# A new hand-out of queues, PSUM banks and alternate engines in a two-layer attention and MLP kernel

## The chip, the cores and the metric

The kernel runs on one core of a Trainium2 chip. A core has a matrix engine (TensorE, PE in the profile; its weight loads are listed apart as PEld), a vector engine (VectorE, DVE), a scalar engine (ScalarE, ACT), GpSimd (POOL) and SyncE (SP), which here only starts transfers. Each engine works through its own queue in the order in which the program filled it; between engines there are only semaphores. Matmul results land in PSUM, which the kernel uses as eight banks of 128 x 512 float32; everything else sits in SBUF.

The metric is the time of one execution on the chip, in microseconds (us).

## The reference

The input is x, 2048 rows of 512 numbers. Two layers follow each other, with the same weights in both, and each layer is

```python
x = x + attention(layernorm(x), wqkv, wo)   # 32 heads of 16, causal, a row sees itself and the 255 rows before it
x = x + gelu(layernorm(x) @ w1 + b1) @ w2 + b2   # 512 -> 1792 -> 512
```

All inputs and the output are bfloat16.

## The kernel before

**Tiling.** Rows are taken in tiles of 128 (tau = 0..31 over both layers) and in blocks of two tiles (b = 0..15; blocks 0 to 7 are the first layer, 8 to 15 the second). A block of the second layer can start as soon as the rows it needs have left the first, so the two layers overlap. The MLP works in ten jobs J of two or four tiles (`JOBS`, line 456): J0 and J1 have two tiles, J2 to J7 four, J8 and J9 two.

**One block of attention.** `lnq` and `kv` (lines 647 and 666) normalize two tiles, transpose them through a DMA, and project them: nodes named `q`, `k`, `v`, whose results leave PSUM through `qe`, `ke`, `ve`. The scores of a block come in ten visits (five in blocks 0 and 8), 150 in all: `sc` (line 740) fills four banks, two `ex` on ACT (line 747) take the exponential of two banks each and write 128 x 1024 into E, and `mk` (line 768) multiplies the edges of the window by a 0/1 mask. After half of the visits, `pv` (line 792) multiplies E by V, with the row sums as a 17th column. Its two banks are transposed to SBUF (`od`, line 801), the sums inverted (`rc`, 805), the rows divided by them (`nm`, 809), transposed again (`ot`, 815), and `op` (the output projection, through line 639) uses the result; `rs` (841) adds it to x. The second half of the visits feeds a second `pv`.

**One MLP job.** `m` nodes multiply by w1. For six of the fourteen columns of tiles the bias is added on DVE (`gb`, line 864) and ACT takes the gelu of two at once (`ga`, 867); for the other eight ACT adds the bias and takes the gelu straight from PSUM (`ge`, 872). `y` nodes multiply by w2; `xb` (880, POOL) and `ya` (884, DVE) add the bias and x.

**Names.** `pv3_1` is the second half of block 3, `sc4_2` is visit 2 of block 4, `y5` the second matmul of the MLP for tile 5. All matmuls against full 128-row weights are recorded under line 639.

**What sets the order.** The program first makes a list of 3080 nodes, in the order in which the lines stand. Three lists written out by hand then decide everything: `_ORDER` is the order in which nodes are put into their engines' queues (SP's DMAs among them), `_ALT` names the nodes that go to their second engine (DVE to POOL for `mk` and `nm`, DVE to ACT for `qe`, `ve`, `te`, POOL to DVE for `vp`), and `_BANKS` gives the PSUM bank of each allocation in turn:

```python
for i in _ALT:
    nodes[i]["eng"], nodes[i]["fn"] = nodes[i]["alts"][1]
for i in _ORDER:
    for g, k in nodes[i]["alloc"]:
        b = next(banks)
        gmap[g] = tuple(range(b, b + k))
```

`_Sched.op` adds the semaphore waits from the reads and writes of each node, bank by bank, so any order that respects them computes the same. Eighteen matmuls on zeros (`warm`, line 532) stand ahead of the first real work.

## Time and profile before

| | us |
|---|---|
| median of 3 runs | 454.1 (453.41 to 454.37) |
| the profiled execution | 453.76 |
| its span, first to last instruction | 451.9 |
| PE busy | 428.1 (95%) |
| ACT busy | 386.4 (85%) |
| DVE busy | 352.2 (78%) |
| POOL busy | 192.2 (43%) |
| PE busy in four stretches: 0 to 100, 100 to 136, 136 to 205, 205 to 452 | 94.85, 25.64, 64.49, 243.16 |

The profiled execution is 0.34 us under the median of the runs shown, and 1.86 us of it lie outside the span. Busy time of PE is counted from the start of a matmul to its modelled end; matmuls overlap, so a PE that is always busy is not yet one that could do no more. Times inside the kernel are counted from the start of the span.

### The profile page before, as it was taken

To read this page: it belongs to the slowest core of one execution; us is meant where nothing else is said; L and a number is where in the kernel's file an instruction comes from. 1 tells how busy PE (TensorE), PEld (TensorE's weight loads), DVE (VectorE), ACT (ScalarE), POOL (GpSimd) and SP (SyncE) were. 2 spreads that over 40 slices of the span, in tenths; PEclk is the share of its full clock that TensorE was granted. 3 is DMA by queue.
4 is the path that set the end of the run, shared out by engine and by line. 5 is a ranking of instruction groups with operands and counts; after the bars stand their busy time and mean duration, and the time that the engine had idled before them with its cause. 6 is when DMAs were issued, how large, how long until landed. Compare 5 with 4: busy or idle time off the path is not lost.

```text
span 451.9 us, 16895 instructions
## 1 busy us (share of the span) xinstructions
PE 428.1 (95%) x7579; PEld 229.2 (51%) x7579; DVE 352.2 (78%) x654; ACT 386.4 (85%) x458; POOL 192.2 (43%) x216
## 2 busy tenths in 40 slices
PE   8998999985879998899999999999999999999997
PEld 4555747543434553445455455455654464444673
DVE  6998699887775778984899877887887598756862
ACT  2998978987799999789998999999878989899633
POOL 4264635236432347632482744364243443526130
PEclk9999999999899999999999999999999999999999
DMA  8684611202300211310022031010232003002110
GB/s 243 190 176 122 166 33 26 43 10 25 82 14 1 24 26 41 73 28 0 15 43 51 0 63 32 10 42 3 64 51 60 1 4 83 10 1 69 60 46 25
DMA packets 47972, 23.25 MB, mean 51 GB/s; under 512 B 33180, under 2 KB 47900, under 8 KB 47900
## 3 DMA queue, kind: packets, MB, share of 16 engines
q1 hardware_dynamic: 47900, 22.17, 21.6%
q8 instruction: 60, 0.98, 1.0%
q14 instruction: 12, 0.10, 0.1%
HBM read 8.00 MB, written 2.10 MB: 22 GB/s over the span
## 4 chain that ended last, share of the span: by engine, by line
PE 73%; ACT 15%; DVE 6%; DMA 3%; issue 1%; SPq 1%; POOL 0%
PE ps L639 57%; ACT E L747 12%; PE ps L740 8%; PE ps L792 7%; DVE E L768 2%; DVE OD L801 1%; DMA Wqkv_sb<-in_A_wqkv_dram 1%; ACT gT L872 1%; DMA xnTA<-xn 1%; DMA xnTB<-xn 1%; ACT gT L867 1%; DVE xn L613 1%; DVE KT L673 0%; DVE stat L591 0%; ACT QT L582 0%
## 5 line engine op out<-in xcount | busy, mean ns | idle before, releaser
L747 ACT ACTIVATE E<-ps 128x1024 bf16<-128x1024 f32 x300 | 283.3, 1040 | 37.6 <-PE ps L740 37.2
L768 POOL TENSOR_TENSOR E<-E,mask 128x512 bf16<-128x512 bf16 (+2 forms) x96 | 103.1, 1088 | 92.4 <-ACT E L747 92.2
L639 PE MATMUL ps<-W_sb,gT 128*128 128x512 bf16 x448 | 118.1, 381 | 0.0
L639 PE MATMUL ps<-xnTB,W_sb 128*128 128x512 bf16 (+1 forms) x560 | 114.6, 337 | 2.4 <-ACT E L747 1.9
L768 DVE TENSOR_TENSOR E<-E,mask 128x512 bf16<-128x512 bf16 (+2 forms) x140 | 70.3, 527 | 10.0 <-ACT E L747 9.8
L639 PE MATMUL ps<-xnTA,Wqkv_sb 128*128 128x256 bf16 x512 | 74.7, 273 | 1.6 <-ACT E L747 0.5
L639 PEld LDWEIGHTS ps<-xnTB,W_sb 128*128 128x128 bf16 x560 | 50.8, 97 | 44.9 <-issue 4.7
L740 PE MATMUL ps<-QT,KT 32*128 32x128 bf16 (+3 forms) x1920 | 60.7, 232 | 8.5 <-DVE OD L801 2.8
L639 PEld LDWEIGHTS ps<-W_sb,gT 128*128 128x128 bf16 x448 | 39.3, 97 | 43.3 <-issue 3.6
L639 PEld LDWEIGHTS ps<-xnTA,Wqkv_sb 128*128 128x128 bf16 x512 | 46.6, 98 | 26.0 <-issue 5.6
L740 PEld LDWEIGHTS ps<-QT,KT 32*128 32x128 bf16 x1920 | 28.9, 93 | 59.5 <-ACT E L747 37.8
L801 DVE STREAM_TRANSPOSE OD<-ps 128x1024 f32<-128x1024 f32 x32 | 39.8, 1245 | 19.6 <-PE ps L792 19.2
L872 ACT ACTIVATE gT<-ps,b1T 128x512 bf16<-128x512 f32 (+1 forms) x80 | 43.5, 609 | 10.2 <-PE ps L639 9.9
L880 POOL TENSOR_TENSOR Xb<-X,b2all 128x512 f32<-128x512 bf16 x32 | 38.5, 1208 | 25.0 <-DVE X L884 25.0
L673 DVE TENSOR_TENSOR KT<-ps,parmask 128x1024 bf16<-128x1024 f32 x32 | 38.8, 1213 | 11.1 <-PE ps L639 10.7
L792 PE MATMUL ps<-E,Va 64*17 64x64 bf16 (+3 forms) x1920 | 41.2, 230 | 4.0 <-ACT E L747 1.7
L591 DVE BATCH_NORM_STATS2 stat<-X 128x6 f32<-128x512 bf16 x64 | 42.7, 677 | 1.9 <-DMA X<-in_A_x_dram 1.8
L864 DVE TENSOR_SCALAR gT<-ps,b1T 128x512 bf16<-128x512 f32 (+1 forms) x60 | 36.6, 630 | 7.6 <-PE ps L639 7.0
L792 PE MATMUL ps<-E,Vs 64*17 64x192 bf16 (+3 forms) x1920 | 42.0, 230 | 0.0
L639 PE MATMUL ps<-Wo_sb,OT 128*128 128x512 bf16 x128 | 39.6, 388 | 1.7 <-DVE OT L815 1.6
L809 POOL TENSOR_TENSOR Nb<-OD,Rc 128x512 bf16<-128x512 f32 x19 | 20.1, 1058 | 48.8 <-DVE Rc L805 40.6
L639 PE MATMUL ps<-Wqkv_sb,xnTA 128*128 128x512 bf16 x128 | 38.6, 385 | 1.3 <-ACT E L747 1.0
(50 smaller groups left out, 354.4 us busy)
## 6 DMA issues: line engine op xcount, KB each, us to landing
Vs<-Va SPq DMA_DIRECT2D x64, 68.0 KB, 2.1
W_sb<-in_B_w_dram SPq DMA_DIRECT2D x4, 512.0 KB, 6.4
out_dram<-X SPq DMA_DIRECT2D x16, 128.0 KB, 1.9
X<-in_A_x_dram SPq DMA_DIRECT2D x3, 512.0 KB, 7.2
Wqkv_sb<-in_A_wqkv_dram SPq DMA_DIRECT2D x4, 256.0 KB, 5.6
W_sb<-in_B_w_dram SPq DMA_DIRECT2D x1, 768.0 KB, 5.5
W_sb<-in_B_w_dram SPq DMA_DIRECT2D x2, 384.0 KB, 3.9
Wqkv_sb<-in_A_wqkv_dram SPq DMA_DIRECT2D x1, 512.0 KB, 7.3
```

Of the source, the lines that this page charges most:

```text
L591: add("dve", lambda e, B, t=t, k6=k6: e.bn_stats(stat6[:, k6, :], X[:, t, :]), reads=["X%d" % t], writes=["st%d" % k6], key="bs%d" % (k + j))
L639: r = e.matmul(ps[:, B[g][0], cols], lhsT, rhs, start=st, stop=sp)
L673: add("dve", lambda e, B, g=g, i=i: e.tensor_tensor(out=KT[:, kb, 2 * i : 2 * i + 2].rearrange("p c m a q -> p a (c m) q"), in0=ps[:, B[g] ...
L740: x = e.matmul(ps[:, bk[r], o : o + n], KT[rows, kb, c, m].rearrange("p a q -> p (a q)"), QT[rows, c, q : q + n], start=True, stop=True)
L747: add("act", lambda e, B, g_=g_, gi=gi: e.activation(E[:, 2 * gi : 2 * gi + 2, e0 : e0 + 512], ps[:, B[g_][0] : B[g_][0] + 2, :], AF.Exp, ...
L768: fn = lambda e, B: e.tensor_tensor(out=Ew, in0=Ew, in1=Mw, op=ALU.mult)
L792: x = e.matmul(ps[32 * r : 32 * r + VW, B[g][par], c % 2 * 2 * P + lo : c % 2 * 2 * P + hi], V[rows, (2 * b + m // 2) % VR, c * HC + 2 * r ...
L801: add("dve", lambda e, B: e.transpose(OD[:, s].rearrange("p a c q -> p (a c q)"), ps[:, B[g][0] : B[g][0] + 2, :]), reads=["ps:" + g], wri ...
L809: return e.tensor_tensor(out=Nb[:, s, :].rearrange("p (k a d) -> p a k d", a=2, d=Dh), in0=sums[:, :, :, 0:Dh], in1=rc[:, :, :, None].to_b ...
L864: add("dve", lambda e, B, g=g, fc=fc: e.tensor_scalar(out=gT[:, fc, c0 : c0 + M], in0=ps[:, B[g][0], 0:M], scalar1=b1T[:, fc : fc + 1], sc ...
L872: add("act", lambda e, B, g=g, fc=fc: e.activation(gT[:, fc, c0 : c0 + M], ps[:, B[g][0], 0:M], AF.Gelu_apprx_tanh, bias=b1T[:, fc : fc + ...
L880: add("pool", lambda e, B, t=t, xs=xs: e.tensor_tensor(out=Xb[:, xs, :], in0=X[:, t, :], in1=b2all[:], op=ALU.add), reads=["X%d" % t, "b2a ...
```

## The change

Only the three lists change; the nodes, their instructions and their shapes are the same. The change is described as giving all queues, banks and alternate engines in a new order, with the ports that VectorE and GpSimd share going to whoever is there first, and the warm-up matmuls keeping to free banks. The diff replaces all of `_ORDER` and `_BANKS` and most of `_ALT`; its first lines:

```diff
 _ORDER = [
-    14, 17, 0, 22, 33, 4, 7, 34, 18, 37, 1, 19, 13, 36, 26, 3, 46, 15, 8, 27, 9, 56, 35, 16, 41, 57, 20, 60, 39, 58,
...
+    14, 17, 22, 0, 4, 33, 34, 37, 18, 19, 26, 36, 46, 35, 7, 41, 1, 15, 13, 3, 8, 9, 27, 56, 57, 60, 58, 59, 61, 2,
...
 _ALT = [
-    60, 66, 74, 79, 108, 112, 120, 125, 164, 169, 184, 191, 210, 219, 336, 341, 369, 373, 377, 378, 383, 392, 397,
...
+    60, 62, 66, 69, 74, 79, 112, 120, 140, 169, 184, 197, 201, 206, 210, 215, 219, 239, 326, 336, 341, 377, 378, 383,
...
 _BANKS = [
-    0, 2, 3, 6, 4, 1, 7, 1, 3, 4, 6, 0, 1, 2, 6, 4, 5, 6, 2, 1, 0, 4, 6, 1, 2, 4, 0, 6, 2, 4, 1, 6, 2, 4, 5, 6, 0, 2,
...
+    0, 7, 2, 0, 4, 6, 1, 6, 7, 0, 2, 5, 4, 6, 0, 5, 0, 6, 2, 4, 5, 2, 0, 7, 4, 2, 0, 6, 2, 4, 0, 6, 2, 5, 4, 6, 0, 2,
...
```

Read as names, and counted by engine:

- PE's queue has the same 1615 nodes, 1501 of them in another place (mean distance 9 places); SP's the same 159, 118 of them in another place. The eighteen warm-up matmuls and the transposes between them stand as before.
- 150 nodes change engine. `mk`: 48 from DVE to POOL, 39 from POOL to DVE. `nm`: 16 from POOL to DVE, 3 back. `vp` (a 128 x 2 addition in the layernorm): 11 from POOL to DVE, 7 back. Evictions of `q`, `v` and `te` from PSUM: 14 from ACT to DVE, 12 from DVE to ACT. DVE then has 664 nodes for 654, POOL 204 for 212, ACT 438 for 440.

As a sample, PE's queue from the first visit of block 3 to the second `pv` of block 4, before (x4 stands for four nodes of one group in a row):

```
sc3_0 y2x7 op5x2 sc3_1 op4x2 y2x3 y3 sc3_2 y3x5 k6_0 sc3_3 y3 k6_0 y3 k6_0 y3 k6_0 sc3_4 y3x2 v11 y3 v10 y3
v10x2 y3 q6_0 sc3_5 v11 v10 v11x2 q6_0 pv3_0 sc3_6 q6_0x2 sc3_7 sc3_8 op6x2 op7x2 sc3_9 q6_1x2 k6_1x3 sc4_0 q6_1
k6_1 q6_1 pv3_1 sc4_1 sc4_2 v12 op7 op6x2 sc4_3 op7 v12x2 sc4_4 v12 v13x2 k7_0 v13 q7_0 v13 k7_0 q7_0 sc4_5
k7_0x2 q7_0x2 pv4_0 sc4_6 m2_3x4 m2_4x2 sc4_7 m2_4 m2_1 m2_4 sc4_8 m2_1x2 m2_5x3 m2_1 m2_5 sc4_9 m2_2x4 sc5_0
sc5_1 pv4_1
```

and after:

```
sc3_0 k5_1x4 y2x3 pv2_1 y2x6 sc3_1 y2x5 sc3_2 op4x4 v10x3 sc3_3 v10 op5x4 sc3_4 q6_0x4 k6_0 sc3_5 k6_0 y3x3
k6_0x2 sc3_6 y3x7 sc3_7 v11x4 pv3_0 sc3_8 q6_1 sc3_9 y3 q6_1 y3x3 q6_1x2 sc4_0 k6_1x4 sc4_1 pv3_1 sc4_2 sc4_3
v12x3 op6 v12 op6x3 sc4_4 op7x4 v13 sc4_5 v13x3 q7_0x4 sc4_6 k7_0x3 sc4_7 k7_0 pv4_0 sc4_8 sc4_9 m2_2x4 m2_5x4
m2_4x2 sc5_0 m2_4x2 m2_3x3 m2_1x4 sc5_1 m2_3 pv4_1
```

## The prediction

> **What bounds the kernel now.** I read the busy times first. PE is busy for 95% of the span and ACT for 85%, so both are candidates and an average can't choose between them.

> ```profile
> PE 428.1 (95%) x7579; PEld 229.2 (51%) x7579; DVE 352.2 (78%) x654; ACT 386.4 (85%) x458; POOL 192.2 (43%) x216
> ```

> Then I read the busy time by windows (length, then PE, PEld, DVE, ACT, POOL busy, granted clock, DMA share, GB/s). They show where PE is not busy.

> ```profile
> 11.30:22.60 11.30, 11.12 (x190) 6.36 (x190) 11.28 (x23) 10.65 (x13) 2.33 (x6) 1.00 0.68 190
> 101.70:113.00 11.30, 6.13 (x200) 3.82 (x200) 8.05 (x14) 8.46 (x10) 7.34 (x8) 1.00 0.21 25
> 113.00:124.30 11.30, 9.28 (x208) 4.90 (x208) 8.59 (x19) 8.54 (x10) 4.74 (x5) 0.85 0.39 83
> 316.40:327.70 11.30, 11.30 (x352) 6.83 (x351) 9.87 (x18) 10.10 (x11) 2.52 (x4) 1.00 0.27 64
> ```

> From 205 us on PE is busy 243.16 of 247 us: there the kernel is at PE's speed. Between about 98 and 135 us, in blocks 3 and 4, no engine is full, and right after it the clock's mean is 0.85. This is a pocket of waits. The chain of waits names them:

> ```profile
> 98.84 7.45 ACT E L747 x8
> 106.31 2.19 DVE E L768 x3
> 111.20 1.17 DVE OD L801
> 114.28 1.33 PE ps L639 x3
> 252.09 9.64 PE ps L639 x44
> ```

> The chain leaves PE, runs through exponentials, masks, the transpose of `pv3_1`, and comes back to PE in `op`. The last line is the other regime: 44 full matmuls in 9.64 us, 0.22 each. The timeline shows the pocket from inside:

> ```profile
> 105.29 2.59 POOL L768 TENSOR_TENSOR E<-E,mask 128x512 bf16<-128x512 bf16 x2
> 106.31 2.19 DVE L768 TENSOR_TENSOR E<-E,mask 128x768 bf16<-128x768 bf16 x3 [2.19 <-ACT E L747]
> 108.60 0.23 PE L792 MATMUL ps<-E,Va 64*17 64x128 bf16 x4 [1.11 <-DVE E L768]
> 112.50 0.40 PE L740 MATMUL ps<-QT,KT 32*128 32x192 bf16 x12 [1.50 <-DVE OD L801]
> 114.28 1.33 PE L639 MATMUL ps<-Wo_sb,OT 128*128 128x512 bf16 x3 [0.83 <-DVE OT L815]
> ```

> One of the three DVE masks ran 1.51 us instead of the usual 0.55: it began under a POOL mask and ended about 0.4 us after it. `pv3_1` waited 1.11 us for it, the next score visit 1.50 for the transpose of `pv3_1`, and `op` 0.83.

> **The change, part by part.**

> *Sums of work.* Prices come from the groups by shape. The net moves are 9 masks from DVE (0.39 to 0.62 us) to POOL (0.70 to 1.66), 13 `nm` from POOL (1.058) to DVE (0.691), 4 `vp` to DVE (0.16) and 2 evictions from ACT (0.61) to DVE (0.68). With the masks' shapes that adds 3.9 us to DVE, 1.7 to POOL and takes 1.2 from ACT. DVE's 3.9 lie beside PE, which is longer everywhere after 205 us; uncovered they would cost 3.9. DVE is full only early (11.28 of 11.3 us above), and up to `od1_0` its queue now holds 30.5 us by these prices against 32.5. I take nothing (0 to 3.9).

> *Entries into tiled matmuls.* When PE goes from a full matmul to `sc` or `pv`, it loses 0.095 us (0.311 between starts for 0.216). The new order has 147 such entries for 154: 0.7 us less. It is counted in the next sum.

> *Score visits.* PE and ACT hand over at 150 visits, and PSUM's eight banks hold two visits at most. So I cut PE's queue at each visit and compare PE's work up to the next (0.216 a full matmul, 0.33 a visit, 1.3 a `pv`, 0.095 an entry) with ACT's work between their exponentials (0.90 each, 0.57 a gelu from PSUM, 0.95 a merged one, 1.28 a table load). The larger counts. Example: between `sc4_1` and `sc4_2` PE has 0.33, ACT two exponentials: 1.8. Before, these sum to 435.7 us; with the first visit at 12.1 that is 447.8, and PE's last matmul really begins at 448.5. The method closes to 1 us. After, the sum is 435.3: a gain of 0.4 (a gain of 3.2 if neighbours are taken in pairs, a loss of 0.5 in threes).

> *The start.* Ahead of the first visit stand 7.7 us of PE work for 8.4, and a statistics instruction (0.68) moves behind the `ke` that the visit needs. Against it, `te1` goes to ACT (0.60 for 0.42). I take a gain of 0.5 (0 to 0.9). The warm-ups keep their places; a wait of theirs would be seen as a gap between them, and there is none: nothing.

> *The pocket.* By the visits, blocks 3 and 4 should take 21.2 + 21.5; they took 21.4 + 25.2. Thus 3.7 us are hand-overs that had too little work behind them. I measured that cover: PE work from the last score of a half to its `pv`, and from `pv` to the first `op` that needs it. Before, in us: `pv3_0` 3.8, `pv3_1` 2.3, `pv4_0` 3.3, `pv4_1` 1.6; `pv3_1` to `op` 0.9. After: 6.1, 3.2, 4.8, 5.3 and 2.0. The first needs two exponentials and a mask, 2.4 us, and more if ACT is behind; `pv3_1` with 2.3 waited 1.1, so it needed about 3.4. The second needs 1.25 + 0.35 + 0.69 + 0.70, so 3.0. What stays short is 0.2 and 1.0: 1.2 of the 3.7. Gain 2.5 (0 to 3.7). The transposes for J2 that SP starts behind `op7` need some 6 us (116.7 to 122.9 before) and get five visits, 9 us.

> *What gets tighter.* `pv7_0` has 2.5 us of cover for 3.4, `pv2_0` 3.5 for 4.9. If 3.4 is needed, 0.9 is lost at `pv7_0`. Four masks that `pv0_1` and `pv1_0` wait for go to POOL, each 0.4 to 1.1 us longer; the cover is 3.6 and 5.9, so I take 0.3 (0 to 6.6, below). 118 moved transfers have the same sizes; SP waits mostly for `xn`, which its order follows. A transfer that comes late shows as a transpose wait on PE, of which the old queue had 0.3 at a time; I take nothing (0 to 2).

> *The ports.* 29 DVE instructions before were stretched, by 17.3 us in all; 23 masks that began under a running POOL instruction ended as it did, plus their own time. [...] By the rows alone, POOL has 105 masks for 96, so at the same rate 17.3 becomes 18.9, off the path but for full stretches. I take nothing (a gain of 1.0, the stretch in the pocket, to a loss of 1.6).

> *Sum.* 453.76 - 0.4 - 0.5 - 2.5 + 0.9 + 0.3 = 451.6 for an execution like the profiled one, which lies 0.34 under the median; on the median 451.9.

> **The rivals.**

> *The pocket stays.* ACT or DVE, not the cover, sets the pocket, and the waits only change places. For it: ACT's busy 7.45 us in a row on the chain. Against it: ACT itself idles 2.8 of 11.3 us there. Then 2.5 are not won: 454.4, no change.

> *Masks on POOL end halves late (slower).* With ACT one visit behind, a half whose last masks are on POOL needs 1.8 + 1.8 + 1.9 = 5.5 us; two behind, 7.3. Of the halves that changed, `pv0_1` has 3.6, `pv1_0` 5.9, `pv5_1` 5.7 with one small mask, `pv15_1` 4.4. Two behind, they lack 3.7, 1.4, 0.4 and, as no visit stands behind `pv15_1`, 1.1 by its gelus: 6.6 us, 458.5. It decides once ACT is more than one visit behind when the last score is issued. For it: ACT is full at 12 to 34 us (10.65 of 11.3). Against it: two visits need all eight banks, which rarely leaves ACT two behind.

> *The pocket closes wholly.* No cover short anywhere, and `pv5_0`, `pv6_0` (8.5 and 7.4 us for 3.8 and 3.9) win some of the 4.5 us that PE idles between 136 and 205: 451.9 - 1.2 - 1.2 = 449.5, less up to 2.

> That the ports collide as often as before, against the change's description, is the loss of 1.6 above; it stays inside the first rival's reach and gets no time of its own.

> **How the numbers follow.** Forecast 0.43, pocket stays 0.17, masks late 0.24, closes wholly 0.16. About 0.2%, 0.9 us, is what a measurement of this kernel can tell from no change. Faster holds the forecast and the last case, 0.59; same 0.15 and slower 0.26, where a little of the second case goes to slower. The range goes from 448, inside the last case, to 458, near the third. The likeliest case alone spans 450.5 to 453.2.

> **What would show it.** Right: fewer than the 10 us that PE idles between 100 and 136; no stretch at half clock there; first score visit before 12.1; entries of `pv3_1` and `op` with waits under 0.5 us. Wrong: PE waiting for `E` from POOL ahead of `pv0_1`, `pv1_0` or `pv5_1`; a new stretch at a lower clock; PE idle over 5 us behind 205, where its sum leaves no room.

## The result, and the profile after

The kernel after takes 464.72 us (464.47 to 465.32), the kernel before, beside it, 453.75 (453.37 to 454.37): a ratio of 1.0242, with an interval of 1.0224 to 1.026. The forecast was 451.9, in a range of 448 to 458, so it was wrong in its sign and in its range. The profiled execution took 464.47 us, with a span of 462.8. Here and below a median is over all executions of a kernel, and a ratio leaves out the few that fell in a slower state (the worst took 636.53 us where the others of its kernel took 504 to 506).

The first part of the page of after (busy time, share of the span, instructions) and the shares of the chain of waits by engine:

```profile
PE 432.5 (93%) x7579; PEld 233.6 (50%) x7579; DVE 359.6 (78%) x664; ACT 386.9 (84%) x456; POOL 194.8 (42%) x208
...
PE 77%; ACT 12%; DVE 5%; issue 4%; DMA 1%; SPq 0%
```

ACT's work is the same, and its share of the chain has fallen from 15% to 12%. DVE and POOL have grown by 7.4 and 2.6 us, and DVE's share of the chain is smaller (5% for 6). "issue" has risen from 1% to 4% of the span: time in which an engine waited for nothing that the profile shows. The busy time by windows of after (columns as in the prediction), in the four stretches of the table above:

```profile
0.00:100.00 100.00, 91.85 (x1496) 55.73 (x1497) 80.97 (x160) 79.26 (x100) 45.81 (x62) 0.97 0.47 115
100.00:136.00 36.00, 28.55 (x656) 14.42 (x654) 28.47 (x55) 28.38 (x31) 13.36 (x14) 0.86 0.24 40
136.00:205.00 69.00, 61.58 (x1263) 31.89 (x1259) 54.48 (x97) 60.37 (x67) 31.71 (x30) 1.00 0.12 24
205.00:463.00 258.00, 250.54 (x4193) 131.58 (x4176) 195.69 (x355) 218.88 (x260) 103.97 (x103) 1.00 0.16 34
```

PE is less busy than before in the first stretch (91.85 for 94.85) and in the third (61.58 for 64.49), and more in the pocket (28.55 for 25.64). The granted clock is 0.97 and 0.86 in the first two stretches, against 1.00 and 0.95. The waits of PE in after (total, times, longest) say on what:

```profile
PE ps L740 <- issue: 8.8, 6, 1.9
PE ps L639 <- issue: 4.6, 4, 1.8
PE ps L740 <- ACT E L747: 4.6, 6, 1.2
```

The waits on "issue" are long ones, ten of them. In before, the first places of this list are ACT's exponentials and DVE's transposes, and no wait of 0.5 us or more is on "issue":

```profile
PE ps L639 <- ACT E L747: 3.4, 5, 1.1
PE ps L740 <- DVE OD L801: 2.8, 5, 1.5
PE ps L639 <- issue: 0.2, 1, 0.2
```

Two places of the timeline of after show what such a wait looks like:

```profile
70.97 0.28 PE L740 MATMUL ps<-QT,KT 32*128 32x256 bf16 x2
73.15 0.39 PE L740 MATMUL ps<-QT,KT 32*128 32x256 bf16 x6 [1.90 <-issue]
...
112.81 0.26 PE L740 MATMUL ps<-QT,KT 32*128 32x192 bf16 x3
114.93 0.58 PE L740 MATMUL ps<-QT,KT 32*128 32x192 bf16 x9 [1.86 <-issue]
```

These are two visits of eight and twelve small matmuls. A visit has its semaphore waits ahead of its first matmul and none inside, and yet PE stops for 1.9 us behind the second and behind the third. No late datum can do that. In both places a `pv` has just ended, as the chain of waits of after shows ahead of the first:

```profile
69.74 1.29 PE ps L792 x96
71.04 0.21 PE ps L740 x2
71.25 1.90 issue
73.15 0.39 PE ps L740 x6
```

Something else in the profile has this rhythm: the queue that brings instructions, in the page's part on DMA queues (packets, MB).

```profile
q8 instruction: 60, 0.98, 0.9%
```

0.98 MB in 60 packets are 16,384 bytes each. PE's records (two for each of the 7579 matmuls, a weight load and the matmul, and 165 others) are 15,323; divided by 256 that is 59.9. So I read each packet as a page of 256 of PE's instructions (an estimate: 15,323 records in 60 packets are 255.4, and 16,384 bytes then make 64 for each). Counted in PE's records from the start of the queue, eight of the ten waits stand at a record whose number is 193 to 195 modulo 256, thus at one and the same place of a page; I call it the edge. Five of them beside the packets' starts, in us (worked out from the records of the trace):

| PE crosses the edge | the next page's packet starts | PE stops at the next edge, and goes on at | from the packet's start |
|---|---|---|---|
| 39.93 | 40.31 | 42.50 (0.95 late) | 2.19 |
| 53.71 | 54.14 | 56.34 (1.12) | 2.20 |
| 69.68 | 70.64 | 73.15 (2.18) | 2.51 |
| 111.52 | 112.46 | 114.93 (2.11) | 2.47 |
| 163.60 | 164.24 | 166.58 (1.60) | 2.34 |

At these stops the packet starts 0.4 to 1.0 us after an edge is crossed, and the next edge isn't passed before 2.2 to 2.5 us after that. (The number in brackets is from matmul to matmul; the profile's wait is 0.2 to 0.4 us less.) So a page took 2.6 to 3.5 us here, though its own work was shorter, and none of the pages from edge to edge took less than 2.57 in after or 3.30 in before. Against full matmuls, 256 instructions are 128 x 0.216 = 28 us (an estimate from the 0.216 us from start to start of a full matmul), and nobody sees it. But a `pv` is 128 small matmuls, a whole page in 1.3 us. Where an edge falls just ahead of a `pv`, the next one comes too early.

*The theory* (I call it instruction pages): the new order puts the page edges of PE's queue at other places of the work, ahead of short stretches; PE stops there; and behind some of the stops the clock is halved. *The rival* is the one that the forecast would have given: it is the order of the data, the placement on engines and their ports that makes the time. The other two waits, at 32.80 and 253.01, are not at an edge (records 67 and 135 modulo 256), and are a cause of their own. Before has a short one at the first of these places (the third line):

```profile
32.80 0.58 PE L639 MATMUL ps<-xnTA,Wqkv_sb 128*128 128x256 bf16 x2 [1.84 <-issue]
253.01 0.59 PE L639 MATMUL ps<-xnTB,W_sb 128*128 128x512 bf16 x2 [0.77 <-issue]
32.70 0.81 PE L639 MATMUL ps<-xnTA,Wqkv_sb 128*128 128x256 bf16 x6 [0.21 <-issue]
```

The first is `q3_1.0`, the first node of after that reads the transpose `tx7`. SP issued `tx7` at 26.69, behind `ldu0`, a third of W1 (512 KB, issued at 24.82), and it landed after 6.0 us, at 32.71; most transposes take 2.4 to 2.5, some up to 4.5. The second is `m4_2.0`, whose transpose landed at 252.92, 4.0 us after its issue. Both go on 0.09 us after the landing, so these are late transposes, although the profile writes "issue". In before, SP's queue has the same order here, and `tx7` lands as late (issued at 26.54, landed at 32.61). But there PE has eight `op` matmuls to do first, which the new order puts behind `q3_1.0`.

The clock: the trace gives after's stretches at 0.5 as 32.8 to 36.2, 73.8 to 77.2, 114.8 to 121.6 and 131.8 to 135.2, 17.1 us in all (what lies at the very end, where PE has no work, is left out here and below). Before had one, 114.4 to 117.9, 3.4 us. Each is 3.413 us or twice that, and each of after's begins within 0.7 us of the end of a long wait. (What PE did ahead of them is in the last section.) A full matmul in them takes 0.427 from start to start, not 0.216.

### The profile page after: what moved, and what is told of

Same layout as the page of the kernel before. It is cut to its first block, busy times and chain, and to the rows that moved or that the text cites. A ratio compares the mean times of both kernels' runs of the same rounds, so it can differ in the third digit from the quotient of the medians.

```text
span 462.8 us, 16906 instructions
## 1 busy us (share of the span) xinstructions
PE 432.5 (93%) x7579; PEld 233.6 (50%) x7579; DVE 359.6 (78%) x664; ACT 386.9 (84%) x456; POOL 194.8 (42%) x208
## 4 chain that ended last, share of the span: by engine, by line
PE 77%; ACT 12%; DVE 5%; issue 4%; DMA 1%; SPq 0%
PE ps L639 60%; ACT E L747 12%; PE ps L740 9%; PE ps L792 7%; PE ps L532 1%; DMA xnTB<-xn 1%; DVE X L841 1%; DVE Nb L809 1%; DVE stat L591 1%; DVE X L884 0%; DVE E L768 0%; DVE xn L613 0%; ACT Va L582 0%; DVE gT L864 0%; PE ps L625 0%
## 5 line engine op out<-in xcount | busy, mean ns | idle before, releaser
L747 ACT ACTIVATE E<-ps 128x1024 bf16<-128x1024 f32 x300 | 284.5, 1033 | 45.6 <-PE ps L740 44.5
L768 POOL TENSOR_TENSOR E<-E,mask 128x512 bf16<-128x512 bf16 (+2 forms) x105 | 120.6, 1159 | 144.5 <-ACT E L747 144.2
L639 PE MATMUL ps<-xnTB,W_sb 128*128 128x512 bf16 (+1 forms) x560 | 112.7, 341 | 2.7 <-issue 2.2
L639 PE MATMUL ps<-W_sb,gT 128*128 128x512 bf16 x448 | 114.2, 380 | 0.0
L639 PE MATMUL ps<-xnTA,Wqkv_sb 128*128 128x256 bf16 x512 | 73.8, 279 | 3.2 <-issue 1.8
L740 PE MATMUL ps<-QT,KT 32*128 32x128 bf16 (+3 forms) x1920 | 62.3, 233 | 15.3 <-issue 8.8
L639 PEld LDWEIGHTS ps<-xnTB,W_sb 128*128 128x128 bf16 x560 | 52.6, 98 | 44.3 <-issue 7.0
L740 PEld LDWEIGHTS ps<-QT,KT 32*128 32x128 bf16 x1920 | 29.1, 93 | 64.4 <-ACT E L747 31.1
L768 DVE TENSOR_TENSOR E<-E,mask 128x512 bf16<-128x512 bf16 (+2 forms) x131 | 57.7, 469 | 4.7 <-ACT E L747 4.5
L639 PEld LDWEIGHTS ps<-xnTA,Wqkv_sb 128*128 128x128 bf16 x512 | 47.8, 100 | 26.2 <-issue 5.9
L639 PEld LDWEIGHTS ps<-W_sb,gT 128*128 128x128 bf16 x448 | 39.8, 98 | 41.8 <-issue 3.4
L801 DVE STREAM_TRANSPOSE OD<-ps 128x1024 f32<-128x1024 f32 x32 | 39.9, 1248 | 15.8 <-PE ps L792 15.3
L864 DVE TENSOR_SCALAR gT<-ps,b1T 128x512 bf16<-128x512 f32 (+1 forms) x60 | 37.6, 637 | 13.0 <-PE ps L639 12.2
L880 POOL TENSOR_TENSOR Xb<-X,b2all 128x512 f32<-128x512 bf16 x32 | 38.4, 1204 | 20.5 <-DVE X L884 14.2
L603 POOL TENSOR_TENSOR rstd<-rstd,mhalf 128x2 f32<-128x2 f32 (+1 forms) x33 | 23.6, 716 | 49.0 <-DVE rstd L597 47.8
L792 PE MATMUL ps<-E,Va 64*17 64x192 bf16 (+3 forms) x1920 | 41.1, 230 | 2.2 <-ACT E L747 1.6
L792 PE MATMUL ps<-E,Vs 64*17 64x192 bf16 (+3 forms) x1920 | 41.7, 230 | 0.4 <-issue 0.4
L639 PE MATMUL ps<-Wo_sb,OT 128*128 128x512 bf16 x128 | 37.7, 397 | 0.5 <-DVE OT L815 0.5
L639 PE MATMUL ps<-Wqkv_sb,xnTA 128*128 128x512 bf16 x128 | 36.1, 389 | 1.3 <-issue 0.6
```

The costliest lines, as they stand in the source:

```text
L603: add("pool", lambda e, B, j=j, n=n: e.tensor_tensor(out=rstd[:, k + j : k + j + n], in0=rstd[:, k + j : k + j + n], in1=mhalf[:, 0:n], op ...
L639: r = e.matmul(ps[:, B[g][0], cols], lhsT, rhs, start=st, stop=sp)
L740: x = e.matmul(ps[:, bk[r], o : o + n], KT[rows, kb, c, m].rearrange("p a q -> p (a q)"), QT[rows, c, q : q + n], start=True, stop=True)
L747: add("act", lambda e, B, g_=g_, gi=gi: e.activation(E[:, 2 * gi : 2 * gi + 2, e0 : e0 + 512], ps[:, B[g_][0] : B[g_][0] + 2, :], AF.Exp, ...
L768: fn = lambda e, B: e.tensor_tensor(out=Ew, in0=Ew, in1=Mw, op=ALU.mult)
L792: x = e.matmul(ps[32 * r : 32 * r + VW, B[g][par], c % 2 * 2 * P + lo : c % 2 * 2 * P + hi], V[rows, (2 * b + m // 2) % VR, c * HC + 2 * r ...
```

## The experiments

An edge is moved through the work by putting more instructions ahead of PE's queue. By cutting PE's queue into pieces at the places where the trace has the edges, and taking each matmul's own time, one can count what the pieces shorter than 3.45 us lack in sum: 14.0 us in after; 5.0 with 208 more instructions in front, 9 less, 21.1 with 152; 3.4 in before, and 20.5 there with 184. Before's 3.4 is near the least that any shift gives it (3.2), and after's 5.0 the least of its own. The 3.45 is an estimate of mine, from the two longest pages of the table (3.47 and 3.41); no run shows it as a least, and the same table has pages of 2.57 and 2.63.

**First four: increments of a semaphore in front.** Between the warm-ups PE increments a semaphore that nobody reads.

```diff
+def warm(e, B, bk=h % 8, n=per[h]):
+    for _ in range(n):
+        e.sem_inc(pad)
+    return e.matmul(ps[:, bk, :], gT[:, 0, 0:P], gT[:, 0, :], start=True, stop=True)
-add("pe", lambda e, B, bk=h % 8: e.matmul(ps[:, bk, :], gT[:, 0, 0:P], gT[:, 0, :], start=True, stop=True),
+add("pe", warm,
     reads=["g0_0", "g0_1"], writes=["ps:init%d" % (h % 8)], key="warm%d" % h)
```

After with 208:

> The kernel after, with 208 semaphore increments that nobody waits for put into PE's queue between the first warm-up matmuls. Order, banks and engines are those of after; only the number that each later PE instruction has in its queue grows by 208. [...] So 464.7 - 9 = 455.7, between 450 (if the stretches at half clock go too) and 457.5 (if the padding costs 1 to 2 at the start). The PE gaps of about 2 us at 71, 113, 164 and 195 us vanish. Rival (order of the data): the gaps come from what PE waits for on other engines and from ports, so nothing but the start changes: 464 to 466, gaps in front of the same nodes.

After with 152:

> As a208 with 152 increments instead. Theory (instruction pages): the pieces then lack 21.1 us instead of 14.0, so slower than after: 464.7 + 7 = 472, between 468 and 477. Rival (order of the data): 464 to 466, no slower than a208.

Before with 184:

> The kernel before, with 184 such increments in PE's queue; nothing else changes. Theory (instruction pages): before lacks only 3.4 us in sum, the least of all shifts; shifted by 184 it lacks 20.5. So 453.75 + 17 = 471, between 465 and 477, with page gaps of 1 to 2.5 us that before doesn't have, each ending 2 to 3 us after the start of a page's transfer. Rival (order of the data): 453.5 to 455.5.

Before with 248, the control:

> Control: the kernel before, with 248 increments, which brings the boundaries to within 8 instructions of where they were (256 is one page). Theory (instruction pages): 3.2 us lacking for 3.4, so 453.5 plus what the padding itself costs at the start, 453 to 456. Rival (order of the data): the same, 453.5 to 456. It prices the padding for the other three.

All four came out above every range that I had set. What I had not reckoned with is the time of the increments: the first projection started 20 to 36 us late, 0.134 to 0.144 us for each. From each time I take what that start lies behind its own kernel's (8.10 in after, 7.78 in before):

| run | median, us | ratio to before | start of the first projection | less its delay |
|---|---|---|---|---|
| after + 208 | 483.67 | 1.0651 (1.0617 to 1.0684) | 37.17 | 454.6 |
| after + 152 | 488.72 | 1.0798 (1.0735 to 1.0861) | 28.45 | 468.4 |
| before + 184 | 506.09 | 1.1139 (1.1099 to 1.1179) | 32.4 to 34.2 (estimate) | 479.6 to 481.5 |
| before + 248 | 489.88 | 1.0794 (1.076 to 1.0827) | 43.38 | 454.3 |

The start of the third is estimated from the other three, by their 0.134 to 0.144 us for each increment. The kernel before beside them took 453.51. The order is what the pages say: after with its best shift is at 454.6, before with a bad one at some 480, and before hardly moves with 248. But the late start also lets loads arrive that had been late (the wait at 32.80 and its half clock are gone in the first), so the correction takes away less than the delay costs or gives. The four point to pages and don't measure them.

**The same shift without the delay.** The 18 warm-ups of 512 columns are replaced by many narrow ones that fill about the same time.

```diff
+def warm(e, B, bk=h % 8, n=6 + (h < 14)):
+    for _ in range(n):
+        r = e.matmul(ps[0:32, bk, 0:72], gT[:, 0, 0:32], gT[:, 0, 0:72], start=True, stop=True)
+    return r
```

122 of 72 columns (208 more instructions), after:

> After, with the 18 wide warm-up matmuls replaced by 122 narrow ones (72 columns instead of 512) that fill about the same time: 208 more instructions stand in front of PE's queue, and nothing else is changed. Instruction pages: the page boundaries fall 208 instructions earlier in the work, where stretches too short for the next page lack 5 us in sum instead of 14, and the half-clock stretches behind the stalls at 71, 113 and 130 us go with them: 456 us (454 to 459); the stall at 31 us, which waits for a transpose, stays. Rival, the order of the data alone (every tile, bank and transfer is where it was): 464.7 us, as the kernel after.

The control, 146 of 60 columns (256 more, a whole page), after:

> The control of the run before: 146 narrow warm-ups (60 columns), 256 more instructions, a whole page, so that the boundaries fall where they fell in the kernel after. Instruction pages: 464.7 us (463 to 466.5), with the stalls at 71 and 113 us in their places. If instead the narrow warm-ups themselves (the clock at the start, the time of the first projection) make the time: as the run with 208, some 456 us.

The other way round, the kernel before with 110 of 80 columns (184 more):

> The kernel before, its order, banks and engines untouched, with 110 narrow warm-ups (80 columns) for the 18 wide ones: 184 more instructions in front. Instruction pages: the short stretches lack 20.5 us instead of 3.4, and some half-clock stretches come with the stalls: 471 us (465 to 478). Order of the data alone: 453.8 us.

These three, and the run below that moves a transfer, stood beside one kernel before of 454.19 us. In the table "page waits" are the waits of PE on "issue" of 0.5 us or more that stand at an edge, so without those for late transposes:

| run | median, us | ratio to before | page waits, us | half clock, us |
|---|---|---|---|---|
| after, as it is (beside 453.75) | 464.72 | 1.0242 (1.0224 to 1.026) | 10.8 | 17.1 |
| after + 256 | 465.31 | 1.0246 (1.02 to 1.0292) | 12.4 | 13.7 |
| after + 208 | 454.86 | 1.0021 (0.9995 to 1.0047) | 2.0 | 3.4 |
| before + 184 | 477.41 | 1.0492 (1.0448 to 1.0537) | 15.0 | 17.1 |

All the page waits of these runs, nine in after + 256, one in after + 208 and ten in before + 184, stand at records 193 to 196 modulo 256; in after it was 193 to 195.

The timeline of after + 256 at the place shown above, now some 2 us later in the run, and of after + 208 at the same visit behind the same `pv`:

```profile
73.29 0.28 PE L745 MATMUL ps<-QT,KT 32*128 32x256 bf16 x2
75.45 0.39 PE L745 MATMUL ps<-QT,KT 32*128 32x256 bf16 x6 [1.88 <-issue]
```

```profile
68.07 0.40 PE L745 MATMUL ps<-QT,KT 32*128 32x256 bf16 x8
68.40 1.70 PE L644 MATMUL ps<-xnTA,Wqkv_sb 128*128 128x256 bf16 x14
```

With a whole page more, PE stops behind the same matmul for the same time. With 208 the eight matmuls run through. The one page stop of 0.5 us or more that is left in that run lies in the middle of a `pv`, as its timeline shows:

```profile
336.14 0.22 PE L797 MATMUL ps<-E,Va 64*17 64x128 bf16 x1
338.39 0.22 PE L797 MATMUL ps<-E,Vs 64*17 64x128 bf16 x6 [2.04 <-issue]
```

And the kernel before, whose order, banks and engines are untouched, becomes 4.9% slower by warm-ups alone. Its waits of PE (total, times, longest) are now led by "issue", with stops as long as those of after:

```profile
PE ps L644 <- issue: 8.6, 37, 1.8
PE ps L797 <- issue: 6.6, 5, 2.5
PE ps L745 <- issue: 6.1, 5, 2.2
```

All three times lie in the ranges of the theory (around 456, 464.7 and 471), and the rival's fail by 10, and by 24 us in the kernel before. That the narrow warm-ups do it by themselves is excluded by the control, whose first projection starts as late (8.72) as that of after + 208 (8.67).

One part of the first expectation missed: the stall for `tx7` did not stay. It is 2.24 us in after + 256 and gone in after + 208, where PE came to `q3_1.0` later (the eight matmuls that end with it begin at 31.83 and run through in 1.05). So the 10.4 us between these two runs are not the pages' alone; some 4 of them can be this stall and its half clock, as the next experiment shows. Before + 184 has no such stall, and there 23 us come with page stops and half clock only.

**The late transfer.** In SP's queue `ldu0` goes behind `tx7`; nothing else moves.

```diff
 tx6
-ldu0
 vs3_0
 vs3_1
 tx7
+ldu0
 ldu1
```

> After, with one transfer moved in SP's queue: the first third of W1 is issued right behind the transpose tx7 and not ahead of it. Late transfer: tx7 lands some 3 us sooner, the stall of 1.84 us at 31 us goes, and with it the half clock from 32.7 to 36.1 us (about 1.7 us): 461.2 us (460 to 463), the page stalls from 71 us on staying. If that stall is covered by a later wait, or the page boundary at 42 us takes the time back: 464.7 us.

460.60 us, a ratio of 1.0154 (1.0117 to 1.0192), against 1.0242: 4 us less. The timeline of this run at `q3_1.0` (the last two matmuls of the second line's eight are those that had waited 1.84):

```profile
30.33 0.41 PE L741 MATMUL ps<-QT,KT 32*128 32x128 bf16 x24
30.67 1.05 PE L640 MATMUL ps<-xnTA,Wqkv_sb 128*128 128x256 bf16 x8
```

The wait is gone, the half clock behind it too (the stretch behind 73 us has gone as well, though its stop of 1.61 us stays), and 11.4 us of page waits remain. In all, half clock fell from 17.1 to 6.8 us. So this is a second, smaller cause, and it adds to the first. It is no transfer that the change had moved: the pair stands in the same order in before.

**Both kernels' page waits out of the way.** Cutting after + 208 at its edges says that from some 240 us on, 240 instructions more would be better than 208. Sixteen 128x512 matmuls of `y13` and `op18` (255 to 265 us) are therefore issued as two of 256 columns, the same work; and the warm-ups get 56 columns, as the first projection had begun 0.5 us later with 72. (That the width did it is not shown: in the run that moved the transfer, with the wide warm-ups, it began at 8.70.)

```diff
 for lhsT, rhs, cols, st, sp in part:
-    r = e.matmul(ps[:, B[g][0], cols], lhsT, rhs, start=st, stop=sp)
+    if st or g not in ("y13", "op18"):
+        r = e.matmul(ps[:, B[g][0], cols], lhsT, rhs, start=st, stop=sp)
+        continue
+    for a in (0, 256):
+        r = e.matmul(ps[:, B[g][0], a : a + 256], lhsT, rhs[:, a : a + 256], start=st, stop=sp and a > 0)
```

> After, with 122 warm-ups of 56 columns (208 more instructions) and, at 255 to 265 us, 16 of the 128x512 matmuls of y13 and op18 each issued as two of 256 columns: from there on 240 more instructions stand in front, at the same work. By the shortfall of the page stretches the stall of 2.04 us at 338 us of the run with 208 goes, and two smaller ones behind it (1 to 2 us), and the narrower warm-ups give back the 0.5 us of its later start: 451.3 us (450 to 453), below the kernel before, and near the 451.9 us that was forecast for the change without its page stalls. If the new order of the data is worth nothing by itself: 453.8 us or more.

With `ldu0` behind `tx7` in addition:

> The same, with the first third of W1 issued behind the transpose tx7 as in the run that moved it alone. There it took 4.1 us, of which the stall of 1.84 us and one half-clock stretch; with the pages moved that stall was no longer there, so it should be worth 0 to 1 us: 450.8 us (449.5 to 452.5). If the transfer is worth as much as alone: 447 us.

The first took 453.14 us beside 454.07 of before, a ratio of 0.9978 (0.9953 to 1.0002), some 2 us over what I expected and just outside the range; the second 451.52, 0.9951 (0.9926 to 0.9976), 0.5% faster than before. The intervals of the two overlap, so what the transfer adds isn't measured by them. The stop at 338 us is gone in both, and in the trace of the first (an execution of 451.86 us) no page wait of 0.5 us or more is left. It still has two late transposes: 0.91 us for `tx7` at 33.28, and 1.39 us at 240.90, which is `m4_2.0` again, 0.09 us after its transpose landed. In the trace of the second `m4_2.0` waits for 1.91 us, and a page stop came where my cut saw none:

```profile
176.03 0.35 PE L802 MATMUL ps<-E,Va 64*17 64x256 bf16 x16
178.78 0.26 PE L802 MATMUL ps<-E,Vs 64*17 64x192 bf16 x4 [2.40 <-issue]
```

The first of the two runs, whose PE queue is the same, has no stop there. (A packet can be late against its edge: in after one started at 172.05, 5.5 us behind the edge at 166.58.) A cut by one length of page is thus good to a few us, not to one. The windows of the first of these runs show the pocket without page waits:

```profile
100.00:136.00 36.00, 30.10 (x805) 16.93 (x805) 32.88 (x63) 33.31 (x37) 13.38 (x15) 1.00 0.26 40
```

**The parts alone.** `_ALT` can be exchanged without `_ORDER` and `_BANKS`: any placement is a correct program. The kernel before with after's `_ALT`:

```diff
-_ALT = [60, 66, 74, 79, 108, ...]   # before's
+_ALT = [60, 62, 66, 69, 74, ...]    # after's
```

> The kernel before with one part of the change alone: the list of alternate engines of the kernel after (PE's queue, its page boundaries, banks and transfers untouched). Instruction pages: PE's instructions and their phase are those of the kernel before, so the loss does not come: 453.8 to 457 us, what is over 453.8 being an order that was not made for these engines. If the placement on VectorE and GpSimd and their shared port carry the loss: 460 us or more.

And the reverse, the run with 208 and 240 (the first of the pair above) with before's `_ALT`:

> The run with 208 and 240 more instructions, with the list of alternate engines of the kernel before: the other part, order and banks, alone and with its page stalls taken out. If the placement of the work on engines is worth little, as the forecast took it: 451 to 455 us. If the new placement is what the new order needs: over 456 us.

484.09 us, 1.0669 (1.0646 to 1.0693), and 493.28 us, 1.0866 (1.084 to 1.0891). Both expectations missed by 27 us and more, each on the side of its rival. So the rival is right in one thing: an order and a placement that don't fit can cost 30 us without page waits. But the loss is not that of the change, since it comes with either list, and is gone where both lists are of one kernel. The busy times of the first, from its page:

```profile
PE 434.2 (90%) x7579; PEld 229.8 (48%) x7579; DVE 372.3 (77%) x664; ACT 387.6 (80%) x456; POOL 196.3 (41%) x208
```

and the waits of PE in it (total, times, longest):

```profile
PE ps L639 <- DVE QT L580: 4.3, 3, 2.3
PE ps L792 <- DVE Va L580: 3.6, 1, 3.6
PE ps L740 <- ACT E L747: 3.5, 8, 0.7
```

There is no page wait of 0.5 us or more (one wait of 0.51 us on "issue" is not at an edge), as PE's queue is before's, and the half clock holds for 10.2 us. DVE is busy 12.7 us more than in after with the same instructions: its masks of 128x768 take 0.667 us each there, 0.550 in after. And PE waits for evictions and masks in many places, up to 3.6 us. So in each kernel the order and the placement fit each other, and exchanging a whole list doesn't take them apart; what the placement is worth by itself is not a number that such a run gives. That the longer waits come from engines that find the next node of their queue not ready, and hold those behind it, is read from the waits and was not tried by itself.

## Why the prediction was wrong

**The step that failed** is the sum of *Score visits*, and with it the whole sum: it takes PE's queue to run at the speed of its instructions whenever data and banks are there. That it "closes to 1 us" on the kernel before was taken for a proof. It closes where before lies at a phase of its pages that costs it nearly nothing (3.4 us by the cut, and no page wait of 0.5 us in its trace, where 184 instructions more cost 23 us on the chip). The term that is missing is PE's stops on "issue": nothing was put for them, and after has 13.4 us of them, 10.8 at page edges and 2.6 for two late transposes. With the pages moved and nothing else changed, after goes from 465.31 to 454.86; 6 to 10 of these 10.4 us are the pages', the rest the stall for `tx7` that went too. The trace of before had the fact, 60 packets on the instruction queue and a `pv` that passes 128 matmuls in 1.3 us. Two waits of before end at an edge, 1.50 us at 112.50 and 1.18 at 190.62, 2.37 and 2.42 us behind a packet's start; but the profile names the transpose of `pv3_1` for the first (it ended 0.14 us before) and an `rc` for the second (it ended just then), and so nothing pointed there.

**A late transfer** was taken at "nothing (0 to 2)", with the moved transfers in mind. `tx7` behind `ldu0` cost 4 us, 1.84 of wait and the rest mostly clock. The place where it would show was named (a transpose wait on PE), but what had moved was its reader and not the transfer: in before it lands just as late and costs 0.21 us, as eight `op` matmuls stand ahead of the reader. So the 0.3 at a time of the old queue is no bound for a new one, and what PE has to do before a landing was a term to count.

**The clock** had no term at all, though the windows of before show 0.85 behind the pocket. It multiplies each stop: 17.1 us at half clock cost up to 17.1 / 2 = 8.5 us of work, in before 1.7. These overlap with waits that would have come anyhow, so stops (13.4) and clock (6.8 more) are more than the 11 us of the result. By the pages of the profile, PE is busy 4.4 us longer in after with the same 7579 matmuls (432.5 for 428.1), and idle 6.5 us longer (30.3 for 23.8); so some 4 us are the clock's, as far as modelled ends tell.

**What held.** *The start:* the first visit began at 11.55 for 12.1, a gain of 0.5, as taken. That is partly luck: from the first projection to the visit it takes 3.45 us for 4.30, and in the run with the transfer moved, where the start is the same, 3.39; but there the projection begins at 8.70, and the visit at 12.09. *The pocket:* in the run without page waits PE idles 5.9 us between 100 and 136 (36 - 30.10), for 10.4 before, and no half clock is left there. `pv3_1` waits 0.52 us for 1.11, the visits behind it 1.13 for 1.50, and `op` not at all for 0.83. In after itself one of the long stops stands in this place, that at 114.93: with 6.8 us of half clock behind it, it took back what the longer cover gave, and 28.55 of 36 is what remained. *Masks on POOL:* in after PE waits for POOL's E in no place for 0.5 us or more; that rival did not come. *The net:* in the run without page waits, the change's order is 0.2% better than before, with an interval that reaches to no change; the forecast had 0.5%. The direction of this part is thus not shown; only the run with the transfer moved too has an interval that lies wholly on the faster side.

**The ports.** DVE's stretched instructions fell from 29 (17.3 us) to 22 (13.3): its masks from 12.2 us to 5.2, against 4.3 more for `nm`. So there are fewer collisions than before, and for `nm` the sum had no term. Seven `nm` of after began with 0.17 to 1.14 us of a POOL mask still to run, and each ended 0.55 us after that mask did; `nm12_1` of before (0.77 us, with 0.22 of a POOL mask left) did too. An `nm` alone takes 0.69, so some 0.14 us of its own time had passed when POOL's mask ended. The masks of before show the same: a held one of 128x768 ended 0.42 us after POOL's and takes 0.55 alone, so "plus their own time" was 0.13 too much. Not all of it was off the path: two of the held `nm`, at 169.44 (1.69 us) and 357.79 (1.67 us), stand on after's chain of waits, each 1.0 us longer than alone. PE waits 0.5 us for the transpose behind the second; what they cost in all is not measured.

**The signs that were named.** "A new stretch at a lower clock" and "PE idle over 5 us behind 205" (7.5 us) were written down as what would show the forecast wrong, and both came. What they would have meant was not asked: as a rival, "something stops PE that is no datum" had no place.

## What to carry to other kernels

Where PE runs many small matmuls in a row, as the 128 of a `pv` in 1.3 us here, count its instructions in the packets that the page lists (256 in each here, by the estimate above). The eight page stops of after ended pages that took 2.6 to 4.0 us from edge to edge, and 208 instructions more, put ahead in the warm-up, left one such stop, where 256, a whole page, had nine. Two versions of such a kernel are then compared at several shifts, or the shift is reckoned out, before anything is said of the edit itself. A wait on "issue" in the middle of a node was the sign of it here; two at the start of a node, at 32.80 and 253.01, were transfers that had landed 0.09 us before, and the landing told. A sum that closes without a term for these stops showed only that this kernel had few of them. And with the stops of after came 17.1 us at half clock.
